# A hand-ordered kernel with two new address forms, first states scaled on another engine, and a new list of tasks

## The chip, the cores and the metric

The kernel runs on one core of one Trainium2 chip. The metric is the device time of one execution in microseconds (us), the median of the runs. A core has five engines that this text names as the profile does: PE (TensorE, matrix products into PSUM), DVE (VectorE), ACT (ScalarE), POOL (GpSimd) and SP (SyncE, which here only issues transfers).

## The reference

For 4 sequences of 768 steps and 8 heads of width 48, a gated state is carried over the steps, and its outputs go through a two-layer product with SiLU:

```python
f = 1.0 / (1.0 + np.exp(-f_logit))
for t in range(S):
    state = f[:, :, t, :, None] * state + np.einsum('bhd,bhe->bhde', k[:, :, t], v[:, :, t])
    y[:, :, t] = np.einsum('bhd,bhde->bhe', q[:, :, t], state)
...
h = x @ w_in                       # x: 3072 x 384 (all heads of y side by side), w_in: 384 x 2048
g = h * (1.0 / (1.0 + np.exp(-h)))
return g @ w_out                   # w_out: 2048 x 384
```

## The kernel before

Each sequence is cut into 6 chunks of 128 steps, so there are 24 units (sequence, chunk). Two units make a pair, and PAIRS lists 12 of them. Pairs 0 to 3 are of the first kind (T): two chunks that follow each other in one sequence, chunks 0 and 1, loaded so that even and odd steps lie side by side. Pairs 4 to 11 (N) are the same chunk of two neighbouring sequences.

The work of a unit `P.i` is a row of tasks, and each has a short name:

- `f`, `q`, `k`, `v`: loads from HBM, issued by SP in the order of the list. `wi`, `wo`: four pieces each of the weights, issued by POOL.
- `E`, `L` (ACT): the logarithm of 1 + exp(-f_logit). `cs` (PE): its cumulative sum. `a`, `ia`, `al` (ACT, L334, L336, L276): exponentials of the sum, of its negative, and of the whole chunk.
- `qg`, `ki` (DVE or POOL, L339): q and k scaled by these. `vb` (L185 or L187): v as bf16.
- `tq` (PE, L346) with `qkc` (a copy, ACT or DVE), or `qkD` (a transposing transfer on SP, L354): both transposed.
- `sc` (PE, L363, L367): the scores of a chunk. `at` (DVE, L371): their triangular mask. `y`, `yi` (PE, L283, L379, L383): the outputs, from the scores and from the state ahead of the chunk.
- `d` (PE, L295, L400): what the chunk adds to the state. `sd` (L404, or a copy for chunk 0, L185, L187): that and the old state. `su` (L414): both scaled by `al`, in two products of 48 partitions by 192 columns, into the new state.
- `yc` (ACT or DVE): y as bf16. `yT` with `xc`, or `yD` (a transposing transfer on SP, L395): y transposed into the tile xT.
- `mi` (PE, L269), `si` (ACT, L274), `mo` (PE, L304), `oc` (ACT or DVE), `so` (SP or POOL): the two layers, SiLU, the copy out of PSUM and the store.
- `idle` (PE, L459): products of zeros.

There is no scheduler at run time. PLAN is a list of words `name:engine:buffers`. The program issues the words from first to last, each on its engine, so every engine works through its own words in order, and waits at a word until the word's operands are there and its buffer or PSUM bank is free. The eight PSUM banks are one class (`pb`), and the number behind a word says which it takes. Whatever stands behind a waiting word on the same engine waits too. The first four loads of the list are issued ahead of the constants.

Whether a first state has a copy of its own is read from the list too: `su` takes its source from `sd` if the list has that word, else from PSUM:

```python
            if ("sd", P, i) in names:
                src = at("sd", P, i)
            else:
                src = at("d", P, i)[:, 0:HD].rearrange("p (n w) -> p n w", w=2 * D)
```

Of the kernel before, what the change touches and what calls it, by code (L numbers as in the profile page):

```python
# [540 lines left out]
```

## Time and profile before

| | |
|---|---|
| median of 3 runs | 186.18 us (183.22 to 188.34) |
| the profiled execution's own time | 181.74 us |
| its span | 179.9 us |
| PE, DVE, ACT, POOL busy | 170.3, 83.2, 134.9, 59.9 us |
| granted TensorE clock, mean | 0.991 |
| read from HBM, written | 25.17 MB, 4.72 MB |

A row of the timeline gives the start, the duration, the engine, the line, the operation, output and inputs, and in brackets the idle time of the engine ahead of it with what ended that. A row of a chain gives the start, the duration and what ran. A row of groups gives how many there were, the busy time, the mean in ns, and the idle time ahead of them. A row of windows gives for each engine the busy time and the number of instructions (PE, weight loads, DVE, ACT, POOL), then the granted clock, the mean share of the 16 transfer engines and GB/s. Two transfers that overlap on one transfer engine can bring a share over 1.

### The profile page before, as it was taken

What the parts mean: (1) busy time and instruction counts of PE and PEld (TensorE: products, weight loads), DVE (VectorE), ACT (ScalarE), POOL (GpSimd) and SP (SyncE); (2) the same over time, 40 slices, a digit from 0 to 9 for tenths busy, and PEclk for the clock granted to TensorE, in tenths of its full rate; (3) what the DMA queues carried; (4) which work ended last, traced back from release to release, by engine and by line L of the source; (5) the groups of instructions that cost most, each with busy time, mean ns of one, the idle gap of its engine ahead of it and who ended that gap; (6) DMA issues with size and microseconds to landing.
All of it is one profiled execution on the core that took longest, in us unless ns stands there. A gap on an engine that the chain in (4) does not pass through costs nothing.

```text
span 179.9 us, 4982 instructions
## 1 busy us (share of the span) xinstructions
PE 170.3 (95%) x2039; PEld 130.0 (72%) x2040; DVE 83.2 (46%) x165; ACT 134.9 (75%) x252; POOL 59.9 (33%) x107
## 2 busy tenths in 40 slices
PE   6978599999999999999999999998999999999992
PEld 2355589998666787679688877787866877887782
DVE  7089977343710263793666064551058758000010
ACT  4899759999936899887997969783896971278321
POOL 6027753695200370140464500581305220003030
PEclk9999879999999999999999999999999999999999
DMA  5999999999989997999949999698985951314043
GB/s 142 315 321 309 202 242 256 230 209 193 180 176 182 203 201 134 210 204 207 158 106 221 178 202 205 125 218 170 216 156 122 213 127 26 109 26 131 0 154 112
DMA packets 109574, 31.91 MB, mean 177 GB/s; under 512 B 103536, under 2 KB 109088, under 8 KB 109552
## 3 DMA queue, kind: packets, MB, share of 16 engines
q1 hardware_dynamic: 104928, 26.19, 69.1%
q0 software_dynamic: 4624, 5.41, 16.0%
q8 instruction: 16, 0.26, 0.6%
q14 instruction: 6, 0.05, 0.1%
HBM read 25.17 MB, written 4.72 MB: 166 GB/s over the span
## 4 chain that ended last, share of the span: by engine, by line
PE 84%; ACT 6%; DVE 3%; DMA 2%; issue 2%; POOL 0%; POOLq 0%; DVEq 0%
PE pb L304 33%; PE pb L269 33%; PE pb L459 3%; DMA xT<-yb 2%; ACT x L334 2%; PE pb L346 2%; PE pb L379 2%; PE pb L383 2%; PE pb L367 2%; DVE atm L371 2%; PE pb L329 2%; DVE qk L339 1%; PE pb L391 1%; PE pb L295 1%; PE pb L363 1%
## 5 line engine op out<-in xcount | busy, mean ns | idle before, releaser
L304 PE MATMUL pb<-w_out_sb,hT 128*128 128x384 bf16 (+1 forms) x416 | 70.7, 313 | 0.1
L269 PE MATMUL pb<-xT,w_in_sb 128*128 128x256 bf16 (+1 forms) x672 | 70.1, 257 | 0.7 <-DMA xT<-yb 0.5
L274 ACT ACTIVATE hT<-pb 128x512 bf16<-128x512 f32 x96 | 51.0, 611 | 23.2 <-PE pb L269 23.1
L269 PEld LDWEIGHTS <-w_in_sb 128*128 128x128 bf16 x672 | 56.9, 98 | 8.2 <-issue 0.9
L304 PEld LDWEIGHTS <-hT 128*128 128x128 bf16 x416 | 37.9, 97 | 18.1
L414 POOL TENSOR_TENSOR st<-sd,al 48x192 bf16<-48x192 f32 x40 | 20.6, 516 | 54.7 <-PE pb L379 18.2
L371 DVE TENSOR_TENSOR atm<-pb,triu 128x512 bf16<-128x512 f32 x32 | 20.0, 682 | 15.2 <-PE pb L367 15.2
L187 DVE COPY ob<-pb 128x384 f32<-128x384 f32 (+1 forms) x16 | 8.3, 526 | 36.0 <-PE pb L304 35.9
L334 ACT ACTIVATE x<-pb 128x384 f32<-128x384 f32 x48 | 22.0, 511 | 3.3 <-PE pb L329 1.5
L507 ACT ACT_TABLE_LOAD x17 | 21.8, 1283 | 0.3
L339 POOL TENSOR_TENSOR qk<-k,x 128x384 bf16<-128x384 f32 x11 | 11.4, 1038 | 14.9 <-DVE vb L187 13.5
L339 DVE TENSOR_TENSOR qk<-k,x 128x384 bf16<-128x384 f32 x13 | 11.9, 936 | 8.3 <-DMA k<-in_k_dram 5.4
L404 DVE TENSOR_TENSOR sd<-pb,st 128x384 f32<-128x384 f32 x16 | 8.6, 550 | 12.6 <-PE pb L400 6.1
L316 POOL DMA_DIRECT2D out_dram<-ob x7 | 4.0, 569 | 29.5 <-ACT ob L185 21.1
L339 DVE TENSOR_TENSOR qk<-q,x 128x384 bf16<-128x384 f32 x17 | 11.4, 688 | 3.3 <-DMA q<-in_q_dram 1.8
L246 ACT ACTIVATE e<-f 128x768 f32<-128x768 f32 (+1 forms) x13 | 10.5, 804 | 2.0 <-DMA f<-in_f_logit_dram 2.0
L185 ACT CAST yb<-pb 128x384 bf16<-128x384 f32 x16 | 7.6, 490 | 3.6 <-PE pb L383 2.4
L371 DVE TENSOR_TENSOR atm<-pb,mask 128x512 bf16<-128x512 f32 x16 | 10.1, 680 | 0.4 <-PE pb L363 0.4
L339 POOL TENSOR_TENSOR qk<-q,x 128x384 bf16<-128x384 f32 x7 | 7.1, 1019 | 7.4 <-ACT x L334 5.8
L459 PE MATMUL pb<-zero,triu 128*128 128x512 bf16 x19 | 7.1, 525 | 1.5 <-POOL triu masks.py:66 1.4
L185 ACT COPY ob<-pb 128x384 f32<-128x384 f32 (+1 forms) x10 | 4.4, 456 | 4.6 <-PE pb L304 4.6
L346 PE MATMUL pb<-ident,qk 128*128 128x128 bf16 x80 | 6.7, 234 | 0.4 <-DVE atm L371 0.4
(72 smaller groups left out, 153.2 us busy)
## 6 DMA issues: line engine op xcount, KB each, us to landing
f<-in_f_logit_dram SPq DMA_DIRECT2D x11, 384.0 KB, 5.5
k<-in_k_dram SPq DMA_DIRECT2D x16, 192.0 KB, 3.7
v<-in_v_dram SPq DMA_DIRECT2D x16, 192.0 KB, 4.3
q<-in_q_dram SPq DMA_DIRECT2D x16, 192.0 KB, 4.2
q<-in_q_dram SPq DMA_DIRECT2D x4, 384.0 KB, 5.2
k<-in_k_dram SPq DMA_DIRECT2D x4, 384.0 KB, 4.9
v<-in_v_dram SPq DMA_DIRECT2D x4, 384.0 KB, 7.3
w_in_sb<-in_moe_w_in_dram POOLq DMA_DIRECT2D x4, 384.0 KB, 7.5
```

Source lines behind the costliest of these rows:

```text
L185: nc.scalar.copy(dst, src)
L246: return nc.scalar.activation(e, at("f", P)[:, j * w:(j + 1) * w], AF.Exp, scale=-1.0)
L269: nc.tensor.matmul(h[:, i, cols], w_in_sb[:, kk, n * 128:(n + 1) * 128], at("xT", P)[:, kk, cols], start=(kk == 0), stop=(kk == KT - 1))
L274: return nc.scalar.activation(at("hT", P)[:, 2 * j:2 * j + 2, :], at("h", P, j).rearrange("p (n c) -> p n c", n=2), AF.Silu)
L304: nc.tensor.matmul(at("o", P, i)[:, cols], at("hT", P)[:, n, i * C:(i + 1) * C], w_out_sb[:, n, cols], start=(n == 0), stop=(n == NT - 1))
L334: nc.scalar.activation(at(kind, P, i).rearrange("p h d -> p (h d)"), at("cs", P, i)[:, 0:HD], AF.Exp, scale=1.0 if kind == "ia" else -1.0)
L339: ENG[eng].tensor_mul(at("qk", P, i)[:, j, :, 0:D], heads("qk"[j], P, i), at("ia" if j else "a", P, i))
L346: nc.tensor.transpose(t_ps[:, j, p, :], at("qk", P, i)[:, j, 2 * p:2 * p + 2, :], ident)
L371: ENG[eng].tensor_mul(at("atm", P, i)[:, r], at(f"s{r}", P, i).rearrange("p (n c) -> p n c", c=C), mask[:, None, :].to_broadcast([C, NP, C]))
L414: ENG[eng].tensor_mul(at("st", P, i)[lo:lo + D, :, r * D:(r + 1) * D], src[lo:lo + D, :, r * D:(r + 1) * D], al_of(P, i)[lo:lo + D, :, Non ...
L459: nc.tensor.matmul(buf["pb", int(got)][:, 0:rest[0]], triu, zero[:, 0:rest[0]], start=True, stop=True, skip_group_check=True)
L507: nc.scalar.preload_act_table_set(TABLES[mode])
```

## The change

The list is new from end to end: the order of the words, the buffers, and for some words the engine. In numbers:

- the four words `sd.0.0`, `sd.1.0`, `sd.2.0`, `sd.3.0` (three ACT, one DVE) are gone, and `su.0.0`, `su.1.0`, `su.2.0`, `su.3.0` go from POOL to DVE, where they read PSUM;
- `ki`: 11 POOL and 13 DVE become 15 and 9; `qg`: 7 POOL and 17 DVE become 15 and 9;
- `vb`: 10 ACT, 6 POOL, 8 DVE become 6, 10, 8; `yc`: 16 ACT, 8 DVE become 11, 13; `xc`: 4 ACT, 8 DVE become 7, 5; `oc`: 10 ACT, 16 DVE become 9, 17;
- the products of zeros are 11, 5, 3 and 1, and become 15, 2, 3 and 4;
- all other words stay, among them 14 `qkD` and 12 `yD`, and every product of PE; ACT changes its table 18 times before and 16 times after.

The beginning of the list, the stretch around pairs 9 and 10, and the two changes in the code:

```diff
-f.0.0:S:0 f.0.1:S: f.2.0:S:1 f.1.0:S:2 q.0.0:S:0 E.0.0:A:0 E.0.1:A: k.0.0:S:0 L.0.0:A:0 L.0.1:A: idle.512.11::0 cs.0.1:P:0 E.2.0:A:1 k.1.0:S:1
-cs.0.0:P:1 ia.0.1:A:0 v.0.0:S:0 E.1.0:A:0 ia.0.0:A:1 q.1.0:S:1 a.0.0:A:2 L.1.0:A:1 qg.0.0:G:0 L.2.0:A:2 f.3.0:S:3 idle.512.5::2 cs.1.1:P:2 ki.0.0:V:
-al.0:A:0 a.0.1:A:3 ki.0.1:V:1 cs.1.0:P:3 ia.1.1:A:4 cs.2.0:P:4 k.2.0:S:2 qg.0.1:V: ia.1.0:A:2 tq.0.0:P:5 ki.1.1:V:2 a.1.0:A:1 cs.2.1:P:6 ki.1.0:V:3
-a.1.1:A:0 q.2.0:S:2 tq.0.1:P:7 vb.0.0:A:0 vb.0.1:V:1 ia.2.1:A:3 qkc.0.1:V:0 d.0:P:1,0 qkc.0.0:A: qg.1.0:V: v.1.0:S:1 qg.1.1:V: sd.0.0:A:0
-idle.512.3::3 sc.0.0:P:3,7 al.2:A:1 ia.2.0:A:4 su.0.0:G:0 sc.0.1:P:5,1 f.4.0:S:0 at.0.0.1:V:0 E.3.0:A:0 at.0.0.0:V: tq.1.0:P:7 al.1:A:2 a.2.0:A:2
-wi.1:G: v.2.0:S:2 at.0.1.0:V:1 tq.1.1:P:2 L.3.0:A:0 qkc.1.1:V:1 qkc.1.0:A: ki.2.1:G:4 idle.512.1::3 cs.3.1:P:3 at.0.1.1:V: cs.3.0:P:4 a.3.1:A:1
-ki.2.0:V:0 wi.0:G: sc.1.0:P:5,2 ia.3.1:A:0 at.1.0.0:V:2 y.0:P:7,1 a.2.1:A:3 qg.2.0:G: al.3:A:3 yc.0.0:A:0 at.1.0.1:V: q.3.0:S:3 sc.1.1:P:6,3
-vb.1.1:A:2 yi.0.1:P: qg.2.1:G: at.1.1.1:V:3 yT.0.0:P:5 vb.1.0:A:3 tq.2.0:P:7 yc.0.1:A:1 at.1.1.0:V: d.1:P:2,3 a.3.0:A:4 wi.2:G: yT.0.1:P:1 sd.1.0:A:1
...
-d.9.0:P:0 y.9.1:P:5 a.10.1:A:2 mo.8.0.3:P: yc.9.1:V:2 y.9.0:P:2 yD.9.1:S:0 oc.8.0:V:5 cs.11.0:P:5 sd.9.0:V:1 mo.8.1.2:P: ia.11.0:A:3 so.8.0:G:
...
+f.2.0:S:0 f.0.0:S:1 f.0.1:S: f.1.0:S:2 q.0.0:S:0 k.0.0:S:0 E.0.0:A:0 E.2.0:A:1 k.1.0:S:1 E.0.1:A: L.0.1:A:0 v.0.0:S:0 L.0.0:A: L.2.0:A:1
+idle.512.15::0 cs.0.0:P:0 E.1.0:A:0 q.1.0:S:1 cs.0.1:P:1 a.0.0:A:0 cs.2.0:P:2 f.3.0:S:3 al.0:A:0 qg.0.0:G:0 ia.0.0:A:1 L.1.0:A:2 ki.0.0:V: wi.1:G:
+ia.0.1:A:2 k.2.0:S:2 idle.512.2::3 cs.1.0:P:3 a.0.1:A:3 cs.1.1:P:4 ki.0.1:V:1 tq.0.0:P:5 qg.0.1:V: ia.1.1:A:4 q.2.0:S:2 qkc.0.0:A:0 vb.0.0:V:0
+ki.1.1:G:2 tq.0.1:P:6 qkc.0.1:V: a.1.1:A:0 v.1.0:S:1 vb.0.1:G:1 ia.2.0:A:1 a.1.0:A:2 qg.1.1:V: idle.512.3::7 sc.0.0:P:7,0 ia.1.0:A:3 cs.2.1:P:1
+at.0.0.0:V:0 qg.1.0:G:3 E.3.0:A:1 sc.0.1:P:5,6 at.0.1.0:V:1 d.0:P:3,7 a.2.0:A:4 ki.1.0:G: ia.2.1:A:0 tq.1.1:P:2 al.2:A:1 a.2.1:A:2 f.4.0:S:0
+qkc.1.1:V:1 tq.1.0:P:5 at.0.1.1:V: qkc.1.0:A: su.0.0:V:0 v.2.0:S:2 ki.2.1:G:4 L.3.0:A:0 at.0.0.1:V: idle.512.4::1 sc.1.1:P:1,2 al.1:A:2 ki.2.0:V:0
+wi.0:G: cs.3.0:P:6 at.1.1.0:V:2 a.3.0:A:3 sc.1.0:P:5,3 qg.2.0:G: y.0:P:0,4 at.1.0.1:V:3 yc.0.0:A:0 yi.0.1:P: cs.3.1:P:1 at.1.1.1:V: qg.2.1:G:
+yc.0.1:A:1 q.3.0:S:3 ia.3.0:A:0 yT.0.0:P:3 at.1.0.0:V: tq.2.0:P:0 xc.0.0:A:0 wi.2:G: yT.0.1:P:4 k.3.0:S:3 vb.1.0:A:2 tq.2.1:P:2 al.3:A:3 xc.0.1:A:
+wi.3:G: vb.1.1:V:3 d.1:P:6,5 ia.3.1:A:1 y.1:P:3,4 su.1.0:V:0 qkc.2.0:A:0 qkc.2.1:V: yi.1.1:P: mi.0.2.1:P:6 yc.1.0:A:2 yc.1.1:V:0 mi.0.2.0:P: a.3.1:A:4
...
+cs.11.1:P:0 y.9.0:P:2 a.11.1:A:3 mi.7.7:P:3 yc.9.0:V:0 ia.11.1:A:1 qg.11.1:G:2 oc.8.0:V:4 cs.11.0:P:0 yD.9.0:S: mo.7.1.1:P: a.11.0:A:0 so.5.1:G:
+ia.11.0:A:4 qg.11.0:V:4 mo.7.1.2:P: vb.10.1:A:4 qkD.10.1:S:0 ki.11.0:G: sc.10.0:P:2,5 at.10.0.1:V:0 mo.7.0.2:P: su.8.0:G:0 qkD.11.0:S:3 at.10.0.0:V:
+mo.8.1.3:P: mi.9.2:P:0 oc.8.1:V:1 ki.11.1:V: y.10.0:P:5 si.9.2:A:2 mi.9.4:P:2 yc.10.0:V:2 si.7.7:A: sd.9.1:V:0 mi.9.5:P:6 su.9.1:G:0 mo.7.1.3:P:
...
                 n = 2 // parts
                 w = n * HD
+                if n == 1:
+                    b, c = us[j][0] - j, us[j][1]
                 src = SRC[kind].rearrange("b h s d -> s (b h) d")[c * C:(c + 1) * C, (b + j * n) * H:(b + (j + 1) * n) * H]
...
         elif kind == "qkD":
-            nc.sync.dma_start_transpose(out=at("qkT", P, i).rearrange("p j n c -> p (j n) c"), in_=at("qk", P, i).rearrange("p j h d -> p (j h d)"))
+            if T:
+                dst = at("qkT", P).rearrange("p j n g s c -> p (j n) g s c")[:, :, :, i]
+            else:
+                dst = at("qkT", P, i).rearrange("p j n c -> p (j n) c")
+            nc.sync.dma_start_transpose(out=dst, in_=at("qk", P, i).rearrange("p j h d -> p (j h d)"))
```

More of the change, by code (lines that the diff above doesn't have):

```diff
@@ new lines @@
+so.1.1:S: mo.2.0.2:P: si.3.3:A: mi.3.6:P:6 f.7.0:S:0 si.3.2:A: mo.2.0.3:P: vb.4.1:A:5 k.7.1:S:2 si.3.4:A: mi.3.0:P:3 oc.2.0:V:3 qkc.4.0:A:1 d.5.0:P:4
+d.4.0:P:5 qkD.5.0:S:2 sd.5.0:V:1 mi.3.7:P:0 sd.4.0:V:0 oc.0.1:A:4 cs.6.0:P:4 si.3.6:A: cs.6.1:P:1 mo.1.0.3:P: si.3.0:A: si.3.7:A: oc.1.0:V:5
+sc.4.0:P:7,5 sc.4.1:P:6,3 at.4.1.0:V:0 mo.3.1.0:P:0 so.1.0:G: qkD.5.1:S:3 at.4.0.0:V:1 d.4.1:P:2 mo.3.1.1:P: a.6.0:A:3 at.4.1.1:V: E.8.0:A:1
+mo.3.0.0:P:6 v.8.0:S:2 at.4.0.1:V: al.6.0:A:1 d.5.1:P:7 E.7.0:A:0 v.9.1:S:3 y.4.1:P:3 mo.3.0.1:P: yc.4.1:V:2 L.8.0:A:2 y.4.0:P:5 al.6.1:A:3
```

111 lines of the change are left out of this document (52 added, 59 removed).

## The prediction

> **What bounds the kernel now.** I read the page first (busy shares, the 40 slices, the chain), then the span in two stretches, then the timeline of each engine in the first 26 us, then the landings of the transfers.
>
> ```profile
> span 179.9 us, 4982 instructions
> PE 170.3 (95%) x2039; PEld 130.0 (72%) x2040; DVE 83.2 (46%) x165; ACT 134.9 (75%) x252; POOL 59.9 (33%) x107
> PE   6978599999999999999999999998999999999992
> PEclk9999879999999999999999999999999999999999
> PE 84%; ACT 6%; DVE 3%; DMA 2%; issue 2%; POOL 0%; POOLq 0%; DVEq 0%
> 0.00:25.20 25.20, 19.53 (x286) 12.36 (x288) 17.46 (x47) 19.58 (x41) 11.07 (x29) 0.93 1.06 259
> 25.20:179.90 154.70, 150.75 (x1758) 117.61 (x1754) 65.70 (x119) 115.37 (x212) 48.87 (x79) 1.00 0.82 164
> ```
>
> TensorE carries 84% of the chain. The two stretches differ: from 25.2 us on it is busy 150.75 of 154.70 us at full clock (most of the rest is the last slice of the row PE, behind the last product), so nothing there can be won but by doing less matrix work, and the change removes none. The first 25.2 us are ragged, the DMA engines are full in them (share 1.06) and the clock is 0.93. So this execution can gain only ahead of the first big product (mi, L269).
>
> ```profile
> 1.38 4.87 PE L459 MATMUL pb<-zero,triu 128*128 128x512 bf16 x11 [1.38 <-POOL triu masks.py:66]
> 6.04 0.85 PE L322 MATMUL pb<-lf,tincl 128*128 128x384 bf16 x2
> 9.88 0.48 PE L322 MATMUL pb<-lf,tincl 128*128 128x384 bf16 x2 [1.19 <-ACT lf L258]
> 21.53 0.48 PE L391 MATMUL pb<-ident,yb 128*128 128x128 bf16 x3 [1.70 <-DVE atm L371]
> 24.66 0.57 PE L283 MATMUL pb<-vb,atm 64*128 64x48 bf16 x32
> 25.17 0.84 PE L269 MATMUL pb<-xT,w_in_sb 128*128 128x128 bf16 x12
> 123.65 6.06 PE L269 MATMUL pb<-xT,w_in_sb 128*128 128x256 bf16 x54 [0.47 <-DMA xT<-yb]
> ```
>
> These are TensorE's waits that matter. The first mi starts at 25.17. The longest wait, 1.70 before 21.53, is behind a VectorE mask product, and its cause stands one instruction earlier on VectorE:
>
> ```profile
> 17.26 0.68 DVE L371 TENSOR_TENSOR atm<-pb,mask 128x512 bf16<-128x512 f32 x1
> 17.86 3.02 DVE L339 TENSOR_TENSOR qk<-k,x 128x384 bf16<-128x384 f32 x1
> 20.80 2.47 DVE L371 TENSOR_TENSOR atm<-pb,mask 128x512 bf16<-128x512 f32 x4
> 18.48 1.97 POOL L339 TENSOR_TENSOR qk<-q,x 128x384 bf16<-128x384 f32 x2
> 11.52 1.02 DVE L339 TENSOR_TENSOR qk<-k,x 128x384 bf16<-128x384 f32 x2
> 138.41 1.35 DVE L339 TENSOR_TENSOR qk<-k,x 128x384 bf16<-128x384 f32 x1
> 138.35 0.99 POOL L339 TENSOR_TENSOR qk<-q,x 128x384 bf16<-128x384 f32 x1
> ```
>
> The scaling of k in ki.2.0 takes 3.02 us on VectorE while GpSimd runs qg.2.0 and qg.2.1 (18.48 to 20.45), and ends 0.43 us after them. The same product takes 0.55 when GpSimd is still (11.52, two in 1.02), and 1.35 beside one GpSimd product (138.41). So a VectorE product of two SBUF operands waits for GpSimd, and here for two products in a row: 3.02 - 0.55 = 2.47 us. Bank 5, which yT.0.0 wants at 21.53, is read by the mask product queued behind it.
>
> The Trainium skill, page "SBUF — State Buffer", section "SBUF: two separate sides", says that VectorE with two SBUF inputs and GpSimd share one port pair that the first to start keeps for its whole instruction. The rows agree on the exclusion; that two GpSimd products can go ahead is in the rows and not in the rule. By the rule alone a collision would cost at most one GpSimd product, about 1.0 us.
>
> **The change part by part.** First, the named edit. Four first states lose their copy out of PSUM (sd, three on ScalarE, one on VectorE) and their two GpSimd products, and get two VectorE products straight from PSUM.
>
> ```profile
> L185 ACT COPY sd<-pb 128x384 f32<-128x384 f32 x3 | 1.5, 512 | 2.2 <-PE pb L295 2.2
> L414 POOL TENSOR_TENSOR st<-sd,al 48x192 bf16<-48x192 f32 x40 | 20.6, 516 | 54.7 <-PE pb L379 18.2 <-DVE sd L404 10.9 <-DVE qk L339 9.1
> L187 DVE COPY ob<-pb 128x192 f32<-128x192 f32 x2 | 0.7, 358 | 21.4 <-PE pb L304 21.4
> 14.68 1.08 POOL L414 TENSOR_TENSOR st<-sd,al 48x192 bf16<-48x192 f32 x2 [4.50 <-ACT al L276]
> 19.49 0.34 PE L379 MATMUL pb<-st,qkTT 128*128 128x96 bf16 x4
> ```
>
> Per state that is 0.51 + 2 x 0.52 = 1.54 us in sequence replaced by two VectorE operations that this trace does not have. The nearest rows bound one by 0.36 (a copy of 192 columns from PSUM) and 0.68 (a mask product of 512 columns with PSUM, at 17.26); I take 0.36, since the columns are 192: 0.7 for both. The saving does not reach the end. State 0 was ready at about 15.8 and its reader yi.0.1 ran at 19.5. In the new list su.0.0 stands on VectorE ahead of at.0.0.1, on which y.0 waits, so the edit by itself puts 0.7 us into the start.
>
> Second, the first loads. f.2.0 (384 KB) goes ahead of f.0.0 and f.0.1 (192 KB each).
>
> ```profile
> 3.27 0.52 ACT L246 ACTIVATE e<-f 128x384 f32<-128x384 f32 x1 [1.25 <-DMA f<-in_f_logit_dram]
> 4.16 0.52 ACT L246 ACTIVATE e<-f 128x384 f32<-128x384 f32 x1 [0.36 <-DMA f<-in_f_logit_dram]
> 4.58 0.92 ACT L258 ACTIVATE lf<-e 128x384 bf16<-128x384 f32 x2
> 5.85 0.84 ACT L246 ACTIVATE e<-f 128x768 f32<-128x768 f32 x1 [0.35 <-DMA f<-in_f_logit_dram]
> 9.58 1.48 DVE L339 TENSOR_TENSOR qk<-k,x 128x384 bf16<-128x384 f32 x2 [5.36 <-DMA k<-in_k_dram]
> L187 DVE COPY qkTT<-pb 128x1024 bf16<-128x1024 bf16 x5 | 3.4, 687 | 3.6 <-PE pb L346 3.6
> 13.33 1.01 DVE L339 TENSOR_TENSOR qk<-q,x 128x384 bf16<-128x384 f32 x2
> 15.71 0.95 POOL L216 DMA_DIRECT2D w_in_sb<-in_moe_w_in_dram  x1
> ```
>
> The three were in by 5.85 at the latest, whatever their order, so the last half of f.0 comes at 5.85 and not at 4.16, and the first cumulative sums move from 6.04 to about 7.6: E.0.1 from 6.2, two L of 0.46, then cs. Fifteen idle products cover that (eleven took 4.87, four more at most 1.8: 8.0). The price is smaller, because ki.0.0 waits for k at 9.58 in any case, and the five transfers ahead of k are the same: what is left is at most the 0.3 us that ki.0.0 then starts later, and it ends in the wait for q below.
>
> Third, wi.1 stands right behind qg.0.0 in GpSimd's queue, so its transfer starts near 10.4 and not at 15.71, among q.1, f.3 and k.2. Between 5.85 and 9.58 three transfers of 384 KB landed, 1.24 us each; one more among them moves q.1 from 13.3 to at most 14.6 (I take 14.4), and qg.1.1, first in VectorE's queue ahead of all masks, with it. The weights come earlier, which nothing in the start waits for.
>
> Fourth, GpSimd gets 30 scalings instead of 18 and VectorE 18 instead of 30. In the start VectorE keeps ki.0.0, ki.0.1, qg.0.1, qg.1.1 and ki.2.0. Behind these in its queue are the masks, for which y and then TensorE wait.
>
> The start then follows VectorE. With no collision: qg.1.1 done at 14.9; two masks 1.2; qkc.1.1 0.7; a mask 0.6; su.0.0 0.7; a mask 0.6: 18.7. Then ki.2.0 0.55, four masks 2.47, and some 1.1 for the cast vb.1.1 (the copy's 0.36), y.1 (24.66 to 25.17) and yi.1.1: first mi at 22.8 instead of 25.17, a gain of 2.4. With one wait of 2.47, as ki.2.0 had, it is 25.3, no gain; qg.2.0 and qg.2.1 follow ki.2.1 on GpSimd again. I take the middle, 24.0: **-1.2 us**. Two waits make it 27.7, +2.5.
>
> Fifth, behind the start. TensorE has the same products there, so only waits can differ. The 0.47 us at 123.65 goes by my reading: the transpose of y.7.1 followed a ScalarE table load and other loads on SP, and the new list puts no table change there and has 7.4 us of TensorE work between y.7 and its mi instead of 6.7: **-0.47**. ScalarE loses some 5 us of work (4 casts of v, 5 of y, 3 states, an output; 3 more of xT), VectorE about 3. Neither bounds, so nothing.
>
> ```profile
> 94.03 0.66 PE pb L269 x6
> 94.68 0.65 PE pb L304 x4
> DMA to landing us min/median/max: 2.3/2.6/5.8
> DMA to landing us min/median/max: 3.0/3.5/5.0
> v<-in_v_dram SPq DMA_DIRECT2D x16, 192.0 KB, 4.3
> q<-in_q_dram SPq DMA_DIRECT2D x16, 192.0 KB, 4.2
> ```
>
> (The two landing lines are those of the tile xT, then of qkT.) With these prices of an mi and an mo word I measured in both lists the TensorE work between y and the first mi. Pair 9 falls from 4.9 to 3.7 us, pair 10 from 4.65 to 3.6, pair 8 grows from 4.8 to 7.6, pair 11 from 4.6 to 5.9. A copy of 0.56 and a median landing of 2.6 need 3.3 with the handovers, so pairs 9 and 10 still fit, with 0.3 to spare; at the longest landing, 5.8, each costs up to 2.8.
>
> The profiled execution took 181.74 us, 1.84 outside its span. Undisturbed the sum is 181.74 - 1.2 - 0.47 = 180.1.
>
> **Late transfers.** The three runs shown took 183.22 to 188.34, median 186.18, that is 4.44 above the profiled one. With TensorE full from 25 us on, I ascribe that to transfers that land later than in the profile; no row shows it. To bound what stays, I compared the work listed between the word of a transfer and its first reader. For qkD it was under the longest landing, 5.0, in 3 of 14 cases and is in none (shortest 4.1, now 5.6). For yD it was under 5.8 in 10 of 12 cases and is in 7. Of the loads for pairs 4 to 11, five stood under 4.2, now three (v.9 moves from 3.3 to 24, q.10.0 from 11.6 to 3.3). 18 exposed transfers become 10; the ends are that all 4.44 stays or none, and I keep half, **+2.2**. Sum: 180.1 + 2.2 = **182.3 us**, 2.1% below the median.
>
> The hunk in the transposing word writes another address pattern only for first-kind pairs, which have no qkD word, and the one in the loads gives the address it gave before, since every split pair has neighbours in the batch: nothing.
>
> **The rivals.** (1) Late transfers hurt as before. For it: 3.6 us for pairs 9 and 10, and that the lateness is inferred. 180.1 + 4.44 = 184.5.
>
> (2) Slower: VectorE is starved in the start. GpSimd's queue there is qg.0.0, ki.1.1, vb.0.1, qg.1.0, ki.1.0, ki.2.1, qg.2.0, qg.2.1, eight operations where there were four, and VectorE has six two-operand or cast operations on the path (ki.0.1, qg.0.1, vb.0.0, qg.1.1, ki.2.0, vb.1.1). Each that waits for two GpSimd products costs 2.47. It decides at three: 22.8 + 7.4 = 30.2, 5.0 later than now, and with all lateness kept 181.74 - 0.47 + 5.0 + 4.44 = 190.7. Against it: GpSimd's products also wait for q.1 and a.1, so they do not all stand back to back, and beside one product the wait was 0.8.
>
> (3) The change doesn't do what it says: one collision eats the start's gain, the transfers shift from one tight place to another, 186.18 - 0.47 = 185.7.
>
> **How the numbers follow.** The forecast has 0.56; its own range is 179.5 to 184.5, and 0.10 of it lies above 182.5. Rival 1 has 0.22, rival 3 0.08, rival 2 0.14. Two per cent, 3.7 us, is about what a measurement of this kernel tells from no change. Faster: 0.46. Within: 0.10 + 0.22 + 0.08 = 0.40. Slower: 0.14. The range runs from 181.74 - 2.4 - 0.47 + 0 = 178.9, taken as 179.0, to two collisions with all the lateness, 181.74 + 2.5 + 4.44 = 188.7, taken as 188.5.
>
> **What the profile after would show.** Right: the first mi between 22.8 and 25.3, ki.2.0 on VectorE well under 3 us, TensorE's waits behind 25 us under 1 us in all, and the runs closer to the profiled time. Wrong: VectorE scalings of 1.3 us and more one after another before 20 us with the first mi past 27; TensorE waiting for xT<-yb at pairs 9 or 10; or runs that spread over 5 us as now.

## The result and the profile after

The changed kernel takes 188.0 us in the median of 20 executions (183.46 to 189.95). The kernel before took 183.71 in the median of 20 executions (181.89 to 188.34), the three shown ahead among them, so their 186.18 was a high draw. The ratio after to before is 1.011, with a 95% interval from 1.008 to 1.015: under 2%, but slower. The ratio leaves out executions more than 1.5% above the fastest of their kernel, which is why it is smaller than the quotient of the medians, 1.023. The forecast was 182.3.

The profiled execution took 185.56 us, span 183.7, against 181.74 and 179.9 before. First the page (span, busy time, TensorE's 40 slices with the granted clock), then the span cut a little after the first mi:

```profile
span 183.7 us, 4986 instructions
PE 171.1 (93%) x2042; PEld 128.7 (70%) x2044; DVE 78.8 (43%) x163; ACT 128.8 (70%) x240; POOL 70.4 (38%) x115
PE   7668889999999999999989999999999999999981
PEclk9999999999999999999999999999999999999999
```
```profile
0.00:24.46 24.46, 18.21 (x295) 11.63 (x298) 14.83 (x47) 19.18 (x40) 13.30 (x30) 1.00 1.04 249
24.46:183.70 159.24, 152.85 (x1750) 117.03 (x1747) 64.00 (x117) 109.58 (x201) 57.10 (x85) 1.00 0.81 162
```

GpSimd carries 70.4 us instead of 59.9, ScalarE and VectorE less, as the list says. The start is shorter, and the clock in it full. The stretch behind it, in which no product was added, is 159.24 us long where before it was 154.70. TensorE's waits in the timeline say where a part of this lies:

```profile
7.73 0.32 PE L324 MATMUL pb<-lf,tincl 128*128 128x384 bf16 x1 [1.65 <-ACT lf L260]
24.13 0.33 PE L385 MATMUL pb<-st,qkTT 128*128 128x96 bf16 x4 [0.48 <-DVE st L420]
24.29 1.17 PE L271 MATMUL pb<-xT,w_in_sb 128*128 128x128 bf16 x18
92.71 0.83 PE L271 MATMUL pb<-xT,w_in_sb 128*128 128x256 bf16 x6 [0.90 <-DMA xT<-yb]
143.01 0.81 PE L271 MATMUL pb<-xT,w_in_sb 128*128 128x256 bf16 x6 [0.33 <-DMA xT<-yb]
161.06 0.81 PE L271 MATMUL pb<-xT,w_in_sb 128*128 128x256 bf16 x6 [0.27 <-DMA xT<-yb]
176.09 1.81 PE L306 MATMUL pb<-w_out_sb,hT 128*128 128x192 bf16 x20 [0.50 <-DVE ob L187]
178.08 1.81 PE L306 MATMUL pb<-w_out_sb,hT 128*128 128x192 bf16 x20 [0.17 <-DVE ob L187]
```

The first mi comes at 24.29 instead of 25.17. Behind it stand three waits for a transposed y (pairs 5, 9 and 11: 1.50 us together, where before there was one of 0.47) and, in the last 8 us, two for a copy out of the bank that the next product wants (0.67). Less the 0.47 of before, these five are 1.7 of the 4.54 us by which the stretch grew. Another 2.1 stand in TensorE's busy time (152.85 us against 150.75): the profile models the ends of products, and a modelled end covers the first part of a wait. Counted instead from the start of one product to the start of the next, against the median interval of each form of product, the five are 3.0 us and the one of before 0.6. And 17 more starts in after come over 0.12 us late, 3.0 us together, against 8 and 1.5 us before. The last 0.6 lie behind the last product: 3.81 us pass from its end to the end of the span, where before 3.17 passed. Call the end of a list, behind the first mi of pair 10, its tail. All nine kernels with the new tail, mended or not, show 3.76 to 3.84 us there, the nine with the old tail 3.12 to 3.19. The new tail stores one of the last two pieces from GpSimd, the old one both from SP; whether that is the reason was not tried.

And on VectorE, the scaling of k for which the prediction feared a collision, and two pairs of the new state products; ahead of them `E.3.0` on ScalarE, which matters below:

```profile
14.65 0.88 ACT L248 ACTIVATE e<-f 128x768 f32<-128x768 f32 x1
17.87 0.71 DVE L420 TENSOR_TENSOR st<-pb,al 48x192 bf16<-48x192 f32 x2
19.23 0.59 DVE L341 TENSOR_TENSOR qk<-k,x 128x384 bf16<-128x384 f32 x1
23.35 0.72 DVE L420 TENSOR_TENSOR st<-pb,al 48x192 bf16<-48x192 f32 x2 [0.87 <-PE pb L297]
```

This execution is one of the shorter ones. 8 of the 20 had a granted clock of 0.996 or more and took 183.46 to 186.06; the 10 below 0.99 took 188.12 to 189.95. So a second loss of some 3 us stands in half of the executions and not in this profile. None of the longer executions was profiled. What they likely lose was found in the profiles of experiments with the same start.

### The profile page after: what moved, and what is told of

Read it like the earlier page. It is cut to its first block, busy times and chain, and to the rows that moved or that the text cites. A ratio compares the mean times of both kernels' runs of the same rounds, so it can differ in the third digit from the quotient of the medians.

```text
span 183.7 us, 4986 instructions
## 1 busy us (share of the span) xinstructions
PE 171.1 (93%) x2042; PEld 128.7 (70%) x2044; DVE 78.8 (43%) x163; ACT 128.8 (70%) x240; POOL 70.4 (38%) x115
## 3 DMA queue, kind: packets, MB, share of 16 engines
HBM read 25.17 MB, written 4.72 MB: 163 GB/s over the span
## 4 chain that ended last, share of the span: by engine, by line
PE 56%; issue 11%; ACT 11%; DMA 10%; SPq 6%; POOL 4%; DVE 0%; POOLq 0%; DVEq 0%; ACTq 0%
PE pb L271 25%; PE pb L306 20%; DMA xT<-yb 6%; SPq L241 5%; ACT L513 4%; DMA k<-in_k_dram 4%; ACT hT L276 3%; POOL qk L341 2%; PE pb L373 2%; PE pb L385 1%; PE pb L389 1%; POOL out_dram L318 1%; PE pb L406 1%; ACT lf L263 1%; PE pb L397 1%
## 5 line engine op out<-in xcount | busy, mean ns | idle before, releaser
L276 ACT ACTIVATE hT<-pb 128x512 bf16<-128x512 f32 x96 | 50.3, 624 | 10.5 <-PE pb L271 10.4
L420 POOL TENSOR_TENSOR st<-sd,al 48x192 bf16<-48x192 f32 x32 | 16.8, 526 | 31.9 <-DVE sd L410 25.2
L341 POOL TENSOR_TENSOR qk<-k,x 128x384 bf16<-128x384 f32 x15 | 15.3, 1026 | 21.6 <-ACT al L338 15.2
L341 POOL TENSOR_TENSOR qk<-q,x 128x384 bf16<-128x384 f32 x15 | 15.3, 1026 | 14.1 <-ACT x L336 8.7
L318 POOL DMA_DIRECT2D out_dram<-ob x9 | 5.1, 563 | 28.5 <-DVE ob L187 14.4
L410 DVE TENSOR_TENSOR sd<-pb,st 128x384 f32<-128x384 f32 x16 | 8.8, 554 | 10.2 <-ACT hT L276 7.3
L248 ACT ACTIVATE e<-f 128x768 f32<-128x768 f32 (+1 forms) x13 | 10.2, 796 | 4.0 <-DMA f<-in_f_logit_dram 4.0
L185 ACT CAST yb<-pb 128x384 bf16<-128x384 f32 x11 | 5.2, 483 | 10.3 <-PE pb L389 7.5
L341 DVE TENSOR_TENSOR qk<-k,x 128x384 bf16<-128x384 f32 x9 | 5.9, 653 | 11.8 <-ACT x L336 8.6
L341 DVE TENSOR_TENSOR qk<-q,x 128x384 bf16<-128x384 f32 x9 | 6.5, 718 | 6.8 <-DMA q<-in_q_dram 3.4
L187 DVE CAST yb<-pb 128x384 bf16<-128x384 f32 x13 | 7.1, 554 | 4.7 <-PE pb L389 3.4
```

Of the source, the lines that this page charges most:

```text
L185: nc.scalar.copy(dst, src)
L187: ENG[eng].tensor_copy(dst, src)
L248: return nc.scalar.activation(e, at("f", P)[:, j * w:(j + 1) * w], AF.Exp, scale=-1.0)
L276: return nc.scalar.activation(at("hT", P)[:, 2 * j:2 * j + 2, :], at("h", P, j).rearrange("p (n c) -> p n c", n=2), AF.Silu)
L341: ENG[eng].tensor_mul(at("qk", P, i)[:, j, :, 0:D], heads("qk"[j], P, i), at("ia" if j else "a", P, i))
L420: ENG[eng].tensor_mul(at("st", P, i)[lo:lo + D, :, r * D:(r + 1) * D], src[lo:lo + D, :, r * D:(r + 1) * D], al_of(P, i)[lo:lo + D, :, Non ...
```

## The experiments

Sixteen kernels ran. "Over before" is the difference of the medians of one call; n is the number of executions. The intervals are those of the ratio.

| kernel | median us (n) | over before | ratio, 95% interval |
|---|---|---|---|
| after | 188.00 (20) | +4.3 | 1.011, 1.008 to 1.015 |
| e1 named edit alone | 184.69 (12) | +0.6 | 0.999, 0.993 to 1.005 |
| e2 new start, old rest | 186.06 (12) | +2.0 | 0.996, 0.991 to 1.002 |
| e3 old start, new rest | 188.32 (6) | +4.3 | 1.017, 1.011 to 1.023 |
| e4 after, yD.5.0 early | 189.83 (6) | +5.8 | 1.034, 1.030 to 1.038 |
| e5 after, old tail | 187.51 (6) | +3.2 | 1.016, 1.006 to 1.026 |
| e6 after, wi.1 later | 187.42 (6) | +3.1 | 1.022, 1.016 to 1.029 |
| e7 after, E.3.0 later | 185.51 (6) | +1.2 | 1.013, 1.006 to 1.020 |
| e8 before, wi.1 early | 185.39 (6) | +1.1 | none |
| e9 new start with E.3.0 later, old rest | 182.84 (10) | 0.0 | 1.003, 0.999 to 1.007 |
| e10 e7 and the old tail | 184.71 (4) | +1.9 | 1.019, 1.003 to 1.034 |
| e11 before, E.3.0 behind a.2.0 | 182.76 (10) | 0.0 | 1.001, 0.996 to 1.005 |
| e12 e7, all yD early | 186.47 (6) | +4.0 | 1.026, 1.020 to 1.031 |
| e13 e7, two stores later | 188.44 (6) | +4.6 | 1.019, 1.012 to 1.025 |
| e14 e13, mended tail | 187.13 (6) | +3.3 | 1.016, 1.009 to 1.023 |
| e15 e14, vb.2.1 later | 184.17 (12) | +1.4 | 1.007, 1.003 to 1.011 |
| e16 before, vb.2.1 early on VectorE | 183.35 (12) | +0.6 | 1.004, 0.999 to 1.008 |

With 6 executions a median is uncertain by 1 to 2 us, so single steps between neighbouring rows are not read.

**The named edit by itself (e1).** The old list; the four `sd` words give way to `su` on VectorE:

```diff
-sd.0.0:A:0 ... su.0.0:G:0 ... sd.1.0:A:1 ... su.1.0:G:0
+su.0.0:V:0 ... su.1.0:V:0
```

> The list of before with the named edit alone: the four sd words of the first states are gone, and su.0.0 to su.3.0 stand in their places on VectorE and read PSUM. If the loss of the change was made behind the start by the new order (first theory), this is the time of before within 0.5 us, because no reader waited for these states. If the edit itself is to blame (VectorE now carries 0.7 us more per state ahead of the masks), it is 0.7 to 2 us slower than before.

0.6 us by medians, and a ratio of 0.999: no difference that can be measured. The product pair costs 0.72 us (15.80 in its timeline), as estimated. With `su.0.0` gone from GpSimd's queue nothing holds back `wi.1` behind it: the profile has it at 10.62 us instead of 15.71. `f.3.0` then lands at 17.97 (before 14.31), ScalarE idles 2.13 us for it at `E.3.0`, TensorE 1.05 at `tq.1.1`, and the first mi comes at 27.66. So the edit alone can set off the chain that the next experiments take apart.

**Start or rest (e2, e3).** The new list up to the first mi and the old one from there, and the reverse; buffers were given anew behind the cut.

```diff
@@ e2, on after; the old order goes on to the end
 yi.1.1:P:
-mi.0.2.1:P:6 yc.1.0:A:2 yc.1.1:V:0 mi.0.2.0:P: a.3.1:A:4 mi.0.3.0:P:0 sd.1.1:V:0
+a.3.1:A:4 sd.0.1:V:0 mi.0.3.0:P:6 yc.1.0:V:2 mi.0.3.1:P: mi.0.2.0:P:0 yc.1.1:A:0
...
@@ e3, on before; the new order goes on to the end
 sd.0.1:V:0
-mi.0.3.0:P:4 yc.1.0:V:2 mi.0.3.1:P: wi.3:G: qkc.2.1:V: yi.1.1:P: mi.0.2.0:P:5
+wi.3:G: qkc.2.1:V: yi.1.1:P: mi.0.2.1:P:4 yc.1.0:A:2 yc.1.1:V:0 mi.0.2.0:P:
...
```

> The new list up to the first mi, then the words that are left in the order and on the engines of before. First theory (the start gained about 1 us, the loss of about 4.8 us in the profiles lies behind it): 1 us faster than before, span near 179, first mi near 24.5. Rival (the start is to blame: load order, early w_in piece, scalings on GpSimd): as slow as the changed kernel, about 2 us slower than before.

> The list of before up to its first mi, then the words that are left in the order and on the engines of the new list. First theory: slower than the changed kernel by the 1 us that its start gained, span 184 to 185, about 3 us slower than before. Rival (the start is to blame): the time of before.

By medians both halves lose time. The expectation for the start, a gain of about 1 us, was missed: in e2's executions with the full clock (182.40 to 183.26) it is near the kernel before, and its other nine took 185.66 to 189.04. Its profile has a wait that the profile of after has not, and the next kernel shows the same one:

```profile
19.15 1.87 PE L347 MATMUL pb<-ident,qk 128*128 128x128 bf16 x16 [3.33 <-ACT x L335]
```

**The transpose of pair 5 earlier (e4).** This was meant for the wait at 92.71.

```diff
-yc.5.0:V:0 si.4.7:A: so.2.0:S: ... v.7.1:S: ... yD.5.0:S:1
+yc.5.0:V:0 yD.5.0:S:1 si.4.7:A: so.2.0:S: ... v.7.1:S:
```

> The new list with one word moved: yD.5.0 stands right behind yc.5.0, ahead of so.2.0, k.8.0, so.3.0 and v.7.1 in the queue of SP, instead of behind them. If its place in that queue made TensorE wait 0.90 us for xT ahead of pair 5, the first mi of pair 5 starts about 1 us earlier and the time falls by 0.5 to 1.0 us against the changed kernel. If the transfer itself is late whatever its place, nothing changes.

The edit comes at 80 us and cannot touch the start, but the profile shows the start's loss in full. Rows of its timeline (ScalarE, then TensorE), then of its windows, whose last three columns are clock, DMA share and GB/s:

```profile
17.88 0.84 ACT L247 ACTIVATE e<-f 128x768 f32<-128x768 f32 x1 [3.23 <-DMA f<-in_f_logit_dram]
18.63 0.85 ACT L335 ACTIVATE x<-pb 128x384 f32<-128x384 f32 x2
19.15 1.87 PE L347 MATMUL pb<-ident,qk 128*128 128x128 bf16 x16 [3.27 <-ACT x L335]
```
```profile
10.00:12.00 2.00, 1.40 (x20) 1.02 (x19) 1.89 (x3) 1.68 (x4) 1.32 (x2) 1.00 1.16 322
12.00:14.00 2.00, 1.31 (x12) 0.76 (x12) 1.74 (x3) 2.00 (x5) 1.57 (x2) 1.00 0.83 171
14.00:16.00 2.00, 1.82 (x58) 1.44 (x58) 1.69 (x4) 0.65 (x2) 1.66 (x2) 1.00 1.19 198
20.00:22.00 2.00, 2.00 (x13) 1.27 (x12) 1.71 (x4) 0.94 (x2) 1.65 (x2) 0.50 0.96 216
```

The reader should follow it backwards. TensorE waits 3.27 us at `tq.1.1`, for the PSUM bank that `a.2.0` on ScalarE still has to read. ScalarE had been standing for 3.23 us, not at `a.2.0` but at `E.3.0`, the word ahead of it: the load `f.3.0`, issued at 9.73, landed at 17.86. In the profile of after it landed at 14.34, `E.3.0` ran at 14.65, and there was no such wait. And between 12 and 16 us the transfers came in at 171 and 198 GB/s, where the 2 us ahead of that had 322: `wi.1`, issued at 10.39, is in flight there until 17.56. (In after, with `wi.1` from 10.54 to 17.36, it was 308 and 217.) In the profile of before the low rates stand where `wi.1` runs there, 222 and 183 GB/s between 18 and 22 us. After the wait the granted clock falls to 0.50, and the products that follow run at about half their rate for a while (the 16 at 19.15 take 1.87 us, in after 1.05).

The Trainium skill, page "DMA: Bandwidth & Descriptors", section "Queues, rings and completion order", says that each DMA engine takes the queues that have work in turn, a packet at a time. That fits a weight piece which slows the loads beside it; what share it takes the page does not say.

**Taking the links apart (e6, e7, e8, e9, e11).** The piece later, its reader later, the piece early in the old list, and the reader later in the new start with the old rest:

```diff
@@ e6, on after
-wi.1:G: ia.0.1:A:2 ... ki.1.0:G: ia.2.1:A:0
+ia.0.1:A:2 ... ki.1.0:G: wi.1:G: ia.2.1:A:0
@@ e7, on after; e9, the same and the old list from mi.0.2.1 on
-qg.1.0:G:3 E.3.0:A:1 sc.0.1:P:5,6 ... a.2.0:A:4 ... qkc.1.0:A: su.0.0:V:0
+qg.1.0:G:3 sc.0.1:P:5,6 ... a.2.0:A:4 ... qkc.1.0:A: E.3.0:A:1 su.0.0:V:0
@@ e8, on before
-qg.0.0:G:0 L.2.0:A:2 ... a.2.0:A:2 wi.1:G: v.2.0:S:2
+qg.0.0:G:0 wi.1:G: L.2.0:A:2 ... a.2.0:A:2 v.2.0:S:2
@@ e11, on before
-at.0.0.1:V:0 E.3.0:A:0 at.0.0.0:V: tq.1.0:P:7 al.1:A:2 a.2.0:A:2
+at.0.0.1:V:0 at.0.0.0:V: tq.1.0:P:7 al.1:A:2 a.2.0:A:2 E.3.0:A:0
```

> The new list with one word moved: wi.1 stands behind ki.1.0 in GpSimd's queue (issued near 16.4 us) instead of right behind qg.0.0 (10.5). Theory: the piece of w_in holds up the loads for 3 us, f.3.0 then comes at 17.9, E.3.0 waits for it on ScalarE, a.2.0 stands behind E.3.0, and TensorE's tq.1.1 waits 3.3 us for the bank that a.2.0 reads; the clock then falls for one or two windows. So f.3.0 lands before 15, the wait at tq.1.1 is under 1 us in the profile, and the median of all runs falls from 188 by 2 to 4 us, to 184 to 186. If the load is late by itself (as the runs scatter), nothing changes. Price on the other side: the piece may come late for the first mi, up to 1 us.

> The new list with one word moved: E.3.0 stands behind qkc.1.0 on ScalarE, so that a.2.0, ia.2.1, al.2, a.2.1 and qkc.1.0 no longer wait behind it for the load f.3.0; the loads and the weights are issued as in the new list. Theory (the link is ScalarE's order): f.3.0 still comes at 17.9 in some executions, but tq.1.1 does not wait for it, and the median falls by 1 to 3 us. If the link is the load itself through other readers (k.2, q.2, v.1 late), TensorE waits a few us later for those, and the gain is under 1 us.

> The list of before with one word moved: wi.1 stands right behind qg.0.0 in GpSimd's queue (issued near 10.2 us) instead of behind su.0.0 (15.7). Theory (the early piece of the weights is what hurts the start): f.3.0 lands near 17.9 instead of 14.8, the waits of TensorE ahead of the first mi grow by 1 to 2 us, and the time by 0.5 to 2 us against before. If the piece is harmless, the time of before.

> The changed list up to the first mi, with E.3.0 moved behind qkc.1.0 on ScalarE, and the old list from there on. The start alone with E.3.0 in its new place gave 186.06 us, with 3.3 us of waiting at tq.1.1. Theory (the start's loss is f.3.0 read too early in ScalarE's order): 186.06 less about 2.5 = 183.5, level with the kernel before, no wait over 1 us at tq.1.1, and 181 to 182 in executions with the full clock, because the first mi then comes before 24 us. Rival (the early weight piece only delays whichever load is next, so one wait replaces the other): 185.5 to 186.5, with a wait of 1 to 3 us between 18 and 30 us at another product.

> The kernel before with E.3.0 behind a.2.0 instead of ahead of it, nothing else. Theory (the old list issues its early weight piece at 15.7 us, so f.3.0 has landed when ScalarE comes to it): no difference, 183.2 to 184.4, no wait at tq.1.1. Rival (reading f.3.0 early costs the old list too, in some executions, so the changed kernel isn't alone in it): 182 to 183, 1 us or more below the kernel before.

The pair e2 and e9 differs by one word: +2.0 us becomes 0.0 in the median. Their ratios, 0.996 and 1.003, do not show it; the executions do (nine of 12 in e2 at 1.6 us or more over the median of before, none of 10 in e9), and so do the two profiles. In both `f.3.0` is late (17.85 and 18.27), but e9 loses 1.51 us at one place instead of 3.33, and its first mi comes at 25.88 instead of 27.87:

```profile
20.06 0.32 PE L323 MATMUL pb<-lf,tincl 128*128 128x384 bf16 x1 [1.51 <-ACT lf L259]
```

In e7, the whole new list with that word moved, +4.3 becomes +1.2 in the median, while the ratio stays (1.011 and 1.013). In its profile `E.3.0` runs at its new place without a wait, and `tq.1.1` waits 0.3. In exchange TensorE waits 1.20 for `L.3.0`, which stands behind `E.3.0`, where after had 0.33 (rows of the timeline, then the group of `tq` between 13 and 24 us):

```profile
17.73 0.85 ACT L247 ACTIVATE e<-f 128x768 f32<-128x768 f32 x1
19.51 0.32 PE L323 MATMUL pb<-lf,tincl 128*128 128x384 bf16 x1 [1.20 <-ACT lf L259]
```
```profile
L347 PE MATMUL pb<-ident,qk 128*128 128x128 bf16 x32 | 2.5, 220 | 0.3 <-POOL qk L340 0.3
```

e8 puts the same wait into the profile of the old list by moving only `wi.1` (there the reader of the bank behind `E.3.0` is `al.1`); its +1.1 us in the median of six is no more than such a median can err by:

```profile
17.93 0.84 ACT L245 ACTIVATE e<-f 128x768 f32<-128x768 f32 x1 [2.82 <-DMA f<-in_f_logit_dram]
18.89 0.83 PE L345 MATMUL pb<-ident,qk 128*128 128x128 bf16 x8 [2.74 <-ACT al L275]
```

e11 shows that the old list has nothing to gain there. So the profiles show the chain in both directions: `wi.1` early, `f.3.0` late, `E.3.0` holding up ScalarE, a bank not free, TensorE standing.

The early piece does not make `f.3.0` late every time. Of all 18 profiles, five issue `wi.1` at 15.7 to 16.2 us, and there `f.3.0` landed at 14.3 to 15.4. Thirteen issue it at 10.2 to 10.6: in nine of them `f.3.0` landed at 16.6 to 18.8, in four (after, e10, e13, e15) by 14.4. These four are the ones in which its issue began 1.15 to 1.21 us ahead of the piece's; in the nine it was 0.27 to 1.09 us ahead. The issues in the profile of after, then in that of e4, which has the same list up to 80 us:

```profile
9.39 1.33 SPq L241 DMA_DIRECT2D f<-in_f_logit_dram  x1
10.54 0.94 POOL L216 DMA_DIRECT2D w_in_sb<-in_moe_w_in_dram  x1
```
```profile
9.73 1.33 SPq L240 DMA_DIRECT2D f<-in_f_logit_dram  x1
10.39 0.94 POOL L215 DMA_DIRECT2D w_in_sb<-in_moe_w_in_dram  x1
```

So a few tenths of a us between two queues go with the whole loss. No kernel varied that lead by itself, and that it is also what splits the executions of after is likely, not shown.

e6 is a miss. With the piece issued at 16.19 `f.3.0` is in time, and the time hardly falls (+3.1). The loss moves on, at least in the profiled execution, which at 191.04 us is the longest of the six (the others took 186.16 to 187.93):

```profile
29.02 0.84 ACT L247 ACTIVATE e<-f 128x768 f32<-128x768 f32 x1 [2.59 <-DMA f<-in_f_logit_dram]
32.90 0.36 DVE L186 CAST vb<-v 128x384 bf16<-128x384 f32 x1 [3.89 <-DMA v<-in_v_dram]
33.17 1.88 DVE L376 TENSOR_TENSOR atm<-pb,mask 128x512 bf16<-128x512 f32 x3
33.91 3.32 PE L270 MATMUL pb<-xT,w_in_sb 128*128 128x128 bf16 x30 [3.09 <-DVE atm L376]
```

Now `f.4.0` (13.0 us from issue to landing) holds up ScalarE at 29.02, and `v.2.0` holds up VectorE at 32.90, with three masks queued behind the cast `vb.2.1`.

**The rest of the list (e5, e10, e12 to e16).** The new list up to the first mi of pair 10 and the words that are left in their old order, on after (e5) and on e7 (e10):

```diff
@@ e5, on after; e10, on e7
 y.11.1:P:0
-mi.10.2:P:5 yc.11.1:A:2 so.7.0:S: si.9.4:A: yD.11.0:S:3 mi.10.5:P:4 si.10.2:A:1
+so.8.0:G: so.6.0:S: so.7.0:S: si.9.7:A: si.9.4:A: mo.9.1.2:P: mo.9.0.2:P:
...
```

> The new list up to its first mi of pair 10, then the words that are left in the order and on the engines of before. Theory of the tail (two waits of TensorE for copies out of PSUM, 0.67 us in all, a late transpose for pair 11, and the last stores cost some 1.6 us of the new list's loss): 1 to 1.7 us faster than the changed kernel at the same granted clock. If the tail only shows a delay that was made earlier: no change.

> The changed list with E.3.0 behind qkc.1.0, and the old list from the first mi of pair 10 on: the two repairs that each gained by themselves (185.51 and 187.51 against 188.0). Theory (they lie at different places and add up): 185.51 less about 1 = 184.5, and under 0.3 us lost behind 175 us. Rival (what the tail gives is covered by the late loads of the start): 185.5, no gain on E.3.0 alone.

The two waits of the tail are gone in both profiles, and behind the last product 3.18 and 3.19 us pass instead of 3.81, but the medians do not show the sum: e10 stands at +1.9, no lower than e7. The cut has a wait of its own, 0.8 us, in both profiles, and e5's has the loss of the start too (4.29 us at `tq.1.1`). The gain of the tail can't be read from these medians.

Then the transposes, each right behind its `yc`. `yD.5.0` and `yD.10.0` move past transfers as shown, `yD.11.0` and `yD.11.1` past `so.7.0`, the others past none:

```diff
@@ e12, on e7
-yc.5.0:V:0 ... so.2.0:S: ... k.8.0:S: ... so.3.0:S: ... v.7.1:S: ... yD.5.0:S:1
+yc.5.0:V:0 yD.5.0:S:1 ... so.2.0:S: ... k.8.0:S: ... so.3.0:S: ... v.7.1:S:
...
-yc.10.0:V:2 ... qkD.11.1:S:2 ... yD.10.0:S:1
+yc.10.0:V:2 yD.10.0:S:1 ... qkD.11.1:S:2
```

> The changed list with E.3.0 behind qkc.1.0, and all twelve yD words right behind the yc word that they read. This moves yD.5.0 past so.2.0, k.8.0, so.3.0 and v.7.1, yD.10.0 past qkD.11.1 and yD.11.0 and yD.11.1 past so.7.0; the rest moves past no transfer. E.3.0 alone in its new place left 1.2 us over the kernel before (ratio 1.013, 1.006 to 1.020). Theory (that rest lies in transposes of y that SP issues behind other transfers): ratio 1.000 to 1.007, and no wait for xT<-yb over 0.4 us. Rival (the transposes are issued in time and the rest lies in landings that vary, and in the tail): ratio 1.009 to 1.020 as before, and runs that still spread over 4 us.

This theory fell: 1.026, worse than e7. Rows of its timeline and of its chain of waits around pair 5, and SP's queue in the profile of after for comparison:

```profile
96.32 0.81 PE L270 MATMUL pb<-xT,w_in_sb 128*128 128x256 bf16 x6 [1.47 <-ACT x L335]
```
```profile
90.53 3.54 DMA k<-in_k_dram
94.06 0.03 POOLq L340
94.09 0.70 POOL vb L186
94.79 0.97 POOL qk L340
```
```profile
84.52 1.23 SPq L316 DMA_DIRECT2D out_dram<-ob  x2
85.80 1.78 SPq L241 DMA_DIRECT2D k<-in_k_dram  x1
87.68 1.17 SPq L316 DMA_DIRECT2D out_dram<-ob  x2
88.96 0.52 SPq L241 DMA_DIRECT2D v<-in_v_dram  x1
90.01 1.22 SPq L401 DMA_TRANSPOSE xT<-yb  x1
```

In after, the transpose of pair 5 is issued at 90.01 although its operand was ready at 82.9: SP stood behind two stores and two loads, each of which holds its queue for 0.5 to 1.8 us. With the transpose ahead of them `v.7.1` lands at 92.43, in e7 at 91.04 and in after at 92.22. GpSimd stands 4.53 us for it (the chain names `k.7.0`, which lands at 94.06, when GpSimd is already at work), its products behind that cast come late, ScalarE waits for a buffer of theirs, and TensorE 1.47 us for ScalarE. SP issues one transfer behind the other in this stretch, whatever stands first. So the stores were moved behind all of these (e13), and the tail was mended with its own words (e14):

```diff
@@ e13, on e7
-so.2.0:S: sd.5.1:V:0 ... k.8.0:S: ... so.3.0:S: ... v.7.1:S: ... yD.5.0:S:1 d.6.0:P:1
+sd.5.1:V:0 ... k.8.0:S: ... v.7.1:S: ... yD.5.0:S:1 so.2.0:S: so.3.0:S: d.6.0:P:1
@@ e14, on e13
-mo.10.1.3:P: mo.11.1.2.0:P: oc.10.1:A:1 mo.9.1.3:P: ... mo.11.1.3.0:P: ... mo.11.1.0.1:P: oc.11.1.0:V:3
+mo.11.1.2.0:P: ... mo.11.1.3.0:P: mo.10.1.3:P: mo.9.1.3:P: oc.10.1:A:1 ... oc.11.1.0:V:3
...
-mo.11.1.1.1:P: mo.11.0.1.0:P: ... mo.11.0.3.0:P: mo.11.1.2.1:P: oc.11.0.0:V:5 mo.11.0.0.1:P:
+mo.11.0.1.0:P: ... mo.11.0.3.0:P: oc.11.0.0:V:5 mo.11.1.0.1:P: mo.11.1.1.1:P: mo.11.1.2.1:P: mo.11.0.0.1:P:
```

> The changed list with E.3.0 behind qkc.1.0, and so.2.0 and so.3.0 moved behind yD.5.0 on SP's queue, so that k.8.0, v.7.1 and yD.5.0 issue some 2.4 us earlier. Theory (the rest behind the start lies at pair 5, where GpSimd's products wait for v.7.1 and k.8.0 and TensorE for yD.5.0): no wait over 0.3 us between 85 and 100 us, ratio 1.003 to 1.009 instead of 1.013. Rival (pair 5 is but one place that shows now and then): ratio 1.010 to 1.020.

> The kernel with so.2.0 and so.3.0 late, and in the last 3 us of products other banks between a copy out and the next product into its bank: mo.10.1.3 and mo.9.1.3 behind mo.11.1.3.0, and the three products of 11.1 behind mo.11.0.3.0. Theory (the tail's two waits of 0.50 and 0.17 us are lost time): both gone, 0.6 to 0.7 us below the kernel with the late stores alone. Rival (the end then waits for the last store anyway): no difference, under 0.3.

In the profiles both work: TensorE's longest wait for a transposed y is 0.4 us, and in e14 the tail has none. The times do not follow: 1.019 and 1.016. Both profiled executions are the shortest of their six, so what a profile names behind the start need not be what most executions lose. The clue was in e3, whose profile has one large wait (VectorE, then TensorE; the last row is GpSimd in the kernel before):

```profile
25.75 0.69 DVE L376 TENSOR_TENSOR atm<-pb,mask 128x512 bf16<-128x512 f32 x1
31.70 0.36 DVE L186 CAST vb<-v 128x384 bf16<-128x384 f32 x1 [5.26 <-DMA v<-in_v_dram]
31.98 1.88 DVE L376 TENSOR_TENSOR atm<-pb,mask 128x512 bf16<-128x512 f32 x3
32.72 4.00 PE L270 MATMUL pb<-xT,w_in_sb 128*128 128x128 bf16 x36 [4.44 <-DVE atm L376]
```
```profile
28.15 0.50 POOL L187 CAST vb<-v 128x384 bf16<-128x384 f32 x1 [0.99 <-DMA v<-in_v_dram]
```

The new list casts `vb.2.1` on VectorE ahead of three masks; the old list casts it on GpSimd, where a weight piece follows, and so its wait of 0.99 us costs nothing. The same cast stands in the rows of e6. Both kernels issue `wi.1` at 16.19. In the 13 profiles with the early piece `v.2.0` landed by 28.3 us, in that of after at 27.14, and the cast never waited more than 0.06. e15 moves it behind the masks, e16 moves it ahead of them in the old list:

```diff
@@ e15, on e14
-mi.1.2.0:P:4 vb.2.1:V:4 mi.1.2.1:P: at.2.1.1:V: ... at.2.0.0:V:1 ... at.2.0.1:V:
+mi.1.2.0:P:4 mi.1.2.1:P: at.2.1.1:V: ... at.2.0.0:V:1 ... at.2.0.1:V: vb.2.1:V:4
@@ e16, on before
-at.2.1.0:V:0 mi.1.3.1:P:3 ... mi.0.0.1:P:5 vb.2.1:G:4
+at.2.1.0:V:0 vb.2.1:V:4 mi.1.3.1:P:3 ... mi.0.0.1:P:5
```

> The kernel with the late stores and the mended tail, and vb.2.1 moved behind at.2.0.1 on VectorE, so that a late v.2.0 holds up no mask product. Theory (the rest behind the start is v.2.0 landing late in many executions): ratio 1.003 to 1.010 instead of 1.016, and the slowest executions 2 to 3 us shorter than 191.6. Rival (that load is late only in the kernels in which the weight pieces stand elsewhere, and the rest is spread over many places): ratio 1.011 to 1.020.

> The kernel before with vb.2.1 on VectorE right behind at.2.1.0, ahead of three mask products, instead of on GpSimd. In the profile of the kernel before, v.2.0 landed at 28.14 us, and at.2.0.0 ran at 28.64. Theory (a late v.2.0 then holds up mask products and TensorE): 0.5 to 2 us above the kernel before, ratio 1.003 to 1.011, and a wait of TensorE for VectorE of 0.5 us or more between 28 and 36 us. Rival: ratio 0.997 to 1.003, no such wait.

e15 comes down to 1.007 from 1.016, the intervals touching between 1.009 and 1.011. In e16 the shift, 0.6 us, has the expected sign and its interval reaches below 1; in its profile the load was 0.29 us late and TensorE lost nothing to it. So the cast explains the profiles of e3 and e6. That the longer executions of after or of e14 lose time to it was not seen in any profile; e15 makes it possible, no more, and 1.4 us stay unexplained there.

No kernel beat both: e9 and e11 are level with the kernel before.

## Why the prediction was wrong, point by point

**The sum.** In the profiled execution the start gave -0.9 us where -1.2 was forecast, and the rest of the span +4.7 where -0.47 was. The median lies 2.4 us above that execution, for which +2.2 was set. So the term that missed is the fifth, what happens behind the start. That +2.2 comes out so near is luck: it was the half that was to be left of 4.44, and by e2 against e9 some 2 us of lateness lie in the start, where the prediction saw none.

**Behind the start, -0.47, the step that missed most.** The prediction held that only waits can differ there, and counted one. Only waits did differ, but many more of them: counted from start to start, late products make 3.8 of the 4.7 us (2.4 the five long waits less the one of before, the rest the short ones), and the time behind the last product 0.6. What ends the short ones was not followed. Part of it belongs to the two executions that were profiled: from the first mi to the end of the last product 155.6 us pass in after and 151.6 before, in the other profiles with the old order there 151.7 to 154.1 (e1, e2, e8, e9, e11, e16), with the new one 152.8 to 155.7 (e4, e7, e12 to e15).

**The reference point.** It set the late transfers at 186.18 - 181.74 = 4.44 us, from three runs. Over 20 runs the median is 183.71, so all that the old list lost in a typical run was 2.0. Half of the 4.44 was booked as a gain against the shown median that was not there.

**The start, -1.2.** Near for the profiled execution, -0.9, but by luck: -1.2 was the middle of no collision and one. There was none (`ki.2.0` took 0.59 us; in e4 it took 1.66), so rival 2, VectorE starved by GpSimd, did not happen, and for that case the prediction had said 22.8. The missing 1.5 are a late `k.2.0`, on the chain for 7.5 us, and the state `su.1.0`. The reading behind the price was not complete either: before, `ki.2.0` starts at 17.86, 0.62 us ahead of `qg.2.0`, while GpSimd issues `wi.0` (17.67 to 18.46), so its 2.47 us are not two products alone. For other executions the point failed, by the next one.

**wi.1, the step that failed in the start.** It was priced as one more load, 1.24 us on q.1, with the sentence that the weights come earlier, "which nothing in the start waits for". Both halves were wrong. `q.1.0` landed at 13.13 in both kernels. `k.2.0` landed at 18.27 instead of 15.83 even in the profile of after, and at 17.2 or later in all 13 profiles with the early piece; `f.3.0` landed at 16.6 to 18.8 in nine of them. And nobody asked which word reads `f.3.0`, what stands behind it on ScalarE, and whose bank that holds. Where `E.3.0` stands early and `f.3.0` is late, TensorE waits 1.05 us (e1), 2.74 (e8), 3.27 (e4), 3.33 (e2) and 4.29 (e5) at `tq.1.1`; in the median the cost is about 2 us (e2 against e9).

**Engines that are "not the bound".** The prediction counted the moves of casts and copies as nothing since neither ScalarE nor VectorE is full. `vb.2.1`, going from GpSimd to VectorE, is such a move. In e3 and e6 its order on the engine mattered (5.26 and 3.89 us of waiting), not the engine's load; in the profile of after it did not wait.

**Late transfers, +2.2.** The gain did not come: it said that fewer transfers would be exposed (18 to 10), and the executions of after spread over 6.5 us, as before. The count compared TensorE's work between the word of a transfer and its first reader. For the loads it left out pairs 0 to 3, where both late loads of the experiments lie: the same count there, without the products of zeros, gives 2.7 us instead of 3.9 from `f.3.0` to `E.3.0`, and 8.0 instead of 10.8 from `v.2.0` to `vb.2.1`. And a word's place in the list is not its time on SP: `yD.5.0` has 6.2 us of work behind its word, but it was issued 7 us after its operand was ready.

**Pairs 9 and 10, -0.47.** The transpose of pair 7 does no longer show, as said; pair 9, named as tight, waits 0.33 in its place, and pairs 5 and 11, which were not named, 1.17. All five waits together, tail included, are 2.2 us.

**The named edit.** The price of 0.36 us a product was right (0.71 and 0.72 for two). It was set for state 0 alone; `yi.1.1` waited 0.48 us for `su.1.0` at 24.13. And that `su.0.0` on GpSimd had kept `wi.1` back until 15.71 was not seen. In time the edit makes no measurable difference (e1).
